# An attention and GEGLU kernel: GELU from ScalarE's table in two batches, column-tiled matmuls between PV bursts, and normalised inputs transposed by DMA

**Chip, cores, metric.** One core of a Trainium2 chip. The metric is the device time of the whole kernel in microseconds (us), the median over repeated runs. Now and then an execution shows a lower granted TensorE clock and takes over 1.5% longer than the fastest of its kernel; it is called *slow*, the others *fast*.

## The reference

```python
xn = layernorm(x)                      # x: 1 x 2048 x 448, bf16
q, k, v = split(xn @ wqkv)             # 16 heads of 28
o = softmax(q @ k.T * 28 ** -0.5) @ v
h = gelu_tanh(xn @ w_gate) * (xn @ w_up)    # 448 -> 1792
out = x + o @ wo + h @ w_down
```

## The kernel before

The program is written by a scheduler in Python: it keeps a clock for each engine, simulates, and emits instructions in the order that the simulation finds. In the traces here every engine, and the queue of DMA issues of SyncE, keeps to its own list and waits for semaphores (below, TensorE stands 12.85 us at one matmul with scores behind it).

Words used below. Tokens come in four blocks of 512. A *tile* is a 128 x 1024 block of scores (two heads x 512 queries, 128 keys); there are 512. Most are exponentiated by ScalarE (*exps*). A *group* is two tiles that VectorE handles by writing bit patterns (`w`, then four `t`), which TensorE multiplies with V four times instead of once. *PV* is the product with V; it uses TensorE as four column tiles of 32.

The GELU, with its scheduling left out (`# ...` marks cuts everywhere):

```python
# g: evicted gate, gu: up * g, both by VectorE
nc.vector.tensor_mul(a, g, g)
nc.vector.tensor_scalar(out=a, in0=a, scalar1=GC1, scalar2=GC0, op0=ALU.mult, op1=ALU.add)
nc.vector.tensor_mul(a, a, g)
nc.scalar.activation(a, a, AF.Tanh, scale=TANH_SCALE)
nc.vector.tensor_scalar(out=a, in0=a, scalar1=0.5, scalar2=0.5, op0=ALU.mult, op1=ALU.add)
nc.vector.tensor_mul(ht, a, gu)
```

Transposes of the normalised inputs of tokens 512 to 2047, and a projection's matmul:

```python
def g_transpose(t0):                       # two token tiles of 128
    tp = aux_tile([P, NDC, 2 * P], BF16, "tp")
    for j in range(2):
        for c in range(NDC):               # four chunks of 112 features
            nc.tensor.transpose(tp[0:DCH, c, j*P:(j+1)*P], xn[:, c*DCH:(c+1)*DCH], ident[:])
    # ... VectorE: xnT[...] = tp

nc.tensor.matmul(ps[:, sl], lhsT=lhsT, rhs=rhs[:, sl], start=start, stop=stop)   # 128 columns
```

The softmax here doesn't subtract the row's maximum and nothing guards it: scores larger than these inputs give would overflow.

## Time and profile before

| | before |
|---|---|
| time, median of 4 runs | 470.06 us (468.82 to 471.89) |
| span in the profile | 466.5 us |
| first exp starts / last exp ends | 12.0 / 458.8 us |
| exps, tanh, table loads between them | 456, 28, 0 |
| ScalarE's waits between first and last exp | 7.7 us |
| tail after the last exp | 7.7 us |

*Waits* here and in all later tables are worked out from the starts of consecutive ScalarE instructions in the trace: what a step takes beyond 0.904 us for an exp and 0.946 us for a tanh or GELU, the steps that the trace shows when nothing waits. Steps into a table load are left out (four, 0.7 us in all in the changed kernel). They include waits too short for the profile to list.

### The profile page before, as it was taken

The numbers are of one execution on the slowest core, as the hardware profiler recorded it, in microseconds if no ns is written. First come the engines' busy times: TensorE is split into PE (matmuls) and PEld (weight loads), VectorE is DVE, ScalarE is ACT, GpSimd is POOL, SyncE is SP. The second block draws the span as 40 slices with busy tenths as digits, with TensorE's granted clock in tenths as the row PEclk, the third lists the DMA queues.
The fourth block names the chain that finished last, engine by engine and source line by source line (L and its number), as shares of the span: only waits on it lengthen the run. The fifth ranks groups of instructions, "written<-read, shape, count | busy, mean of one in ns | idle before, by whom it ended". The sixth has DMA issues, their size and how long they took to land.

```text
span 466.5 us, 9032 instructions
## 1 busy us (share of the span) xinstructions
PE 442.0 (95%) x3468; PEld 156.5 (34%) x3469; DVE 392.9 (84%) x676; ACT 451.8 (97%) x496; POOL 21.1 (5%) x78
## 2 busy tenths in 40 slices
PE   8899999999999999999899999999999899998985
PEld 4333334333223333333233333333233233322431
DVE  6787789789999988999999976899999996697253
ACT  4999999999999999999999999999999999999994
POOL 5602030000000000000000000000000000000000
PEclk9999999999999999999999999999999999999999
DMA  6920112022101002030221000121202100020001
GB/s 161 303 67 2 41 36 64 22 60 59 43 7 39 11 15 57 4 100 22 60 61 42 0 12 21 53 68 52 60 21 54 29 11 12 12 52 1 3 1 39
DMA packets 41051, 20.70 MB, mean 44 GB/s; under 512 B 8240, under 2 KB 41008, under 8 KB 41008
## 3 DMA queue, kind: packets, MB, share of 16 engines
q1 hardware_dynamic: 40112, 19.68, 15.7%
q8 instruction: 27, 0.44, 0.4%
q10 hardware_dynamic: 896, 0.44, 0.3%
q14 instruction: 16, 0.13, 0.1%
HBM read 18.09 MB, written 1.84 MB: 43 GB/s over the span
## 4 chain that ended last, share of the span: by engine, by line
PE 57%; DVE 26%; ACT 8%; issue 4%; DMA 2%; POOL 1%; ACTq 0%; DVEq 0%; SPq 0%; POOLq 0%
PE st L588 15%; PE gups L306 14%; PE ot L636 11%; PE op L306 10%; ACT e L600 7%; DVE w L610 5%; PE pp L306 4%; DVE t L628 4%; DVE gl L394 3%; DVE gu L435 3%; PE pv L306 3%; DVE g L430 3%; DVE otsb L658 2%; DVE w L628 2%; DMA x<-in_A_x_dram 2%
## 5 line engine op out<-in xcount | busy, mean ns | idle before, releaser
L600 ACT ACTIVATE e<-st 128x1024 bf16<-128x1024 f32 x456 | 425.2, 1148 | 2.2 <-PE st L588 2.0
L588 PE MATMUL st<-qT,kT 28*128 28x512 bf16 x1024 | 132.4, 383 | 9.1 <-ACT e L600 7.3
L610 DVE TENSOR_SCALAR w<-st 128x1024 f16<-128x1024 f32 x56 | 68.2, 1219 | 15.6 <-PE st L588 15.0
L588 PEld LDWEIGHTS <-kT 28*128 28x128 bf16 x1024 | 39.0, 91 | 124.4 <-issue 120.3
L636 PE MATMUL ot<-e,va 128*32 128x512 bf16 x912 | 72.5, 383 | 1.3 <-ACT e L600 0.5
L306 PE MATMUL gups<-xnT,wg 112*128 112x512 bf16 (+1 forms) x232 | 62.0, 374 | 1.4 <-DVE kT L343 0.7
L306 PE MATMUL gups<-xnT,wu 112*128 112x512 bf16 (+1 forms) x226 | 61.4, 379 | 2.0 <-DVE qT L343 0.6
L628 DVE TENSOR_SCALAR t<-w 128x2048 uint16<-128x2048 f16 x84 | 54.4, 678 | 0.1
L306 PE MATMUL op<-wd_sb,ht 128*128 128x448 bf16 (+1 forms) x233 | 51.5, 347 | 0.1
L636 PEld LDWEIGHTS <-va 128*32 128x32 bf16 x1360 | 31.1, 95 | 50.8 <-issue 34.9
L430 DVE CAST g<-gups 128x512 bf16<-128x512 f32 x56 | 38.4, 686 | 5.3 <-PE gups L306 4.7
L435 DVE TENSOR_TENSOR gu<-gups,g 128x512 bf16<-128x512 f32 x56 | 38.1, 684 | 2.4 <-PE gups L306 2.1
L413 ACT ACTIVATE gl<-gl 128x1024 bf16<-128x1024 bf16 x28 | 32.9, 1174 | 0.0
L658 DVE TENSOR_TENSOR otsb<-ot,otsb 128x512 f32<-128x512 f32 x36 | 24.6, 684 | 7.1 <-PE ot L636 6.8
L636 PE MATMUL ot<-t,va 128*32 128x512 bf16 x336 | 29.7, 383 | 0.4 <-DVE t L628 0.2
L306 PEld LDWEIGHTS <-wg 112*128 112x128 bf16 x232 | 19.0, 97 | 30.9 <-issue 18.4
L306 PEld LDWEIGHTS <-wu 112*128 112x128 bf16 x226 | 18.3, 97 | 30.8 <-issue 18.8
L306 PEld LDWEIGHTS <-ht 128*128 128x128 bf16 x233 | 19.2, 98 | 24.5 <-issue 12.3
L628 DVE TENSOR_SCALAR w<-w 128x2048 uint16<-128x2048 f16 x28 | 19.3, 690 | 0.7
L394 DVE TENSOR_TENSOR gl<-gl,g 128x1024 bf16<-128x1024 bf16 x28 | 19.2, 685 | 0.3
L394 DVE TENSOR_TENSOR gl<-g 128x1024 bf16<-128x1024 bf16 x28 | 19.1, 684 | 0.2
L394 DVE TENSOR_TENSOR ht<-gl,gu 128x1024 bf16<-128x1024 bf16 x28 | 19.1, 683 | 0.2
(105 smaller groups left out, 289.8 us busy)
## 6 DMA issues: line engine op xcount, KB each, us to landing
wg<-in_B_w_gate_dram SPq DMA_DIRECT2D x28, 224.0 KB
wu<-in_B_w_up_dram SPq DMA_DIRECT2D x28, 224.0 KB
out_dram<-res SPq DMA_DIRECT2D x15, 112.0 KB
wd_sb<-in_B_w_down_dram SPq DMA_DIRECT2D x1, 1568.0 KB
x<-in_A_x_dram SPq DMA_DIRECT2D x3, 448.0 KB
den<-otsb SPq DMA_DIRECT2D x60, 2.0 KB
rr<-recb SPq DMA_DIRECT2D x60, 1.0 KB
wst<-in_A_wqkv_dram SPq DMA_DIRECT2D x2, 392.0 KB
```

What stands on the lines that cost most here:

```text
L306: nc.tensor.matmul(ps[:, sl], lhsT=lhsT, rhs=rhs[:, sl], start=start, stop=stop, skip_group_check=True)
L394: (nc.gpsimd if eng == "POOL" else nc.vector).tensor_mul(out, a, b)
L413: nc.scalar.activation(st["a"][:], st["a"][:], AF.Tanh, scale=TANH_SCALE)
L430: nc.vector.tensor_copy(g[:, k, :], ps[:])
L435: nc.vector.tensor_mul(gu[:, k, :], ps[:], g[:, k, :])
L588: nc.tensor.matmul(st[:, j * QT : (j + 1) * QT], lhsT=kT[(hg, kc // 4)][32 * hh : 32 * hh + Dh, (kc % 4) * P : (kc % 4 + 1) * P], rhs=qT[( ...
L600: nc.scalar.activation(e[:], s_tiles.pop(k)[:], AF.Exp, scale=SCALE)
L610: nc.vector.tensor_scalar(out=w_tiles[g][1][:, 2 * i * QT : 2 * (i + 1) * QT], in0=s_tiles.pop(k)[:], scalar1=128.0 * SCALE * LOG2E, scala ...
L628: nc.vector.tensor_scalar(out=bits, in0=w[:], scalar1=c, scalar2=None, op0=ALU.add)
L636: nc.tensor.matmul(ot[32 * hh : 32 * hh + 32, :], lhsT=va, rhs=rhs, start=(b, hh) not in started, stop=last, tile_position=(0, 32 * hh), s ...
L658: nc.vector.tensor_add(otsb[:], ot[:], otsb[:])
```

## The change

The intent: ScalarE has a GELU, so five VectorE instructions per pair of gate tiles can go; two batches keep the switches of ScalarE's table few; VectorE has time for more groups, ScalarE for fewer exps. Matmuls that follow a PV burst are issued as four column tiles, so that TensorE need not change its mode. And TensorE and VectorE are freed of the transposes of tokens 512 on. The core of the diff:

```diff
+    def f(k, ps): nc.vector.tensor_copy(ht[:, k, :], ps[:])             # gate
+    def f(k, ps): nc.vector.tensor_mul(ht[:, k, :], ps[:], ht[:, k, :]) # up, after the GELU
+    for Q in BATCHES[batch_i[0]]:          # BATCHES = ((0, 1), (2, 3)), 14 activations each
+        for pr in range(NPR):
+            nc.scalar.activation(ht[:], ht[:], AF.Gelu_apprx_tanh)
-    # the chain around tanh
@@ matmuls
+            for m in range(0, P, P // cols):          # cols is 4 next to a PV burst, else 1
+                nc.tensor.matmul(ps[m : m + P // cols, sl], lhsT=lhsT[:, m : m + P // cols], ...,
+                                 **({"tile_position": (0, m)} if cols > 1 else {}))
@@ transposes
-            add(first - 8 + k, [...], lambda t0=t0: g_transpose(t0))
+    def ln_apply_t(t):
+        ln_apply(t)
+        for c in range(NDC):
+            nc.sync.dma_start(xnT[T][:, c, j * P : (j + 1) * P], xn[:, c * DCH : c * DCH + P], transpose=True)
+        xt_at[t] = clock["DVE"] + T_XT     # T_XT = 6000: the scheduler counts on them 6 us later
@@ norms: 1/denominator is broadcast by a DMA through HBM, not by a matmul
@@ limits of the groups
-    D_SLACK = 5; D_END = 2; D_STOP = 40; NL = 6
+    D_SLACK = 20; D_END = 3; D_STOP = 60; NL = 8
```

## The prediction

> **What bounds the kernel now.** I read the head of the page first, then its 40 slices. The columns of the first part are the engine, busy time, share of the span and instructions.
>
> ```profile
> span 466.5 us, 9032 instructions
> PE 442.0 (95%) x3468; PEld 156.5 (34%) x3469; DVE 392.9 (84%) x676; ACT 451.8 (97%) x496; POOL 21.1 (5%) x78
> ...
> DVE  6787789789999988999999976899999996697253
> ACT  4999999999999999999999999999999999999994
> ```
>
> ScalarE is full in every slice but the first and the last. TensorE at 95% looks as full, but its busy time is a union of modelled, overlapping spans; the slices do not tell which of the two sets the pace. So I turned to the timeline of ScalarE (start, length, engine, line, operation, count, and idle time before in brackets).
>
> ```profile
> 11.96 3.77 ACT L600 ACTIVATE e<-st 128x1024 bf16<-128x1024 f32 x4 [0.61 <-PE st L588]
> ...
> 200.72 1.20 ACT L413 ACTIVATE gl<-gl 128x1024 bf16<-128x1024 bf16 x1
> 201.67 16.75 ACT L600 ACTIVATE e<-st 128x1024 bf16<-128x1024 f32 x18
> ...
> 219.07 3.04 ACT L600 ACTIVATE e<-st 128x1024 bf16<-128x1024 f32 x3
> 221.78 1.26 ACT L413 ACTIVATE gl<-gl 128x1024 bf16<-128x1024 bf16 x1
> ...
> 424.65 34.14 ACT L600 ACTIVATE e<-st 128x1024 bf16<-128x1024 f32 x37
> 461.98 0.97 ACT L1292 CAST res<-fa 128x448 bf16<-128x448 f32 x2 [3.18 <-PE fa L1283]
> ```
>
> Start to start gives what an instruction costs when the next follows at once. Three exps take 221.78 - 219.07 = 2.71 us, so 0.903 us each; a tanh takes 201.67 - 200.72 = 0.95 us. The first exp starts at 11.96 and the last ends at 424.65 + 34.14 = 458.79. Between lie 456 exps x 0.903 = 411.8 us and 28 tanh x 0.95 = 26.6 us, 438.4 of 446.8 us. So **ScalarE's instruction count sets the time**: 12.0 us of prologue, 438.4 of work, 8.4 of waits (many under the 0.2 us that the views show as idle), 7.7 of tail. A TensorE that stood in the way would leave more than 2% of waits.
>
> VectorE already takes exps from ScalarE. A group handles two score tiles by writing bit patterns: two w instructions from PSUM, then four terms, each of which TensorE multiplies again. The groups of instructions by line (busy time, mean ns | idle) are:
>
> ```profile
> L610 DVE TENSOR_SCALAR w<-st 128x1024 f16<-128x1024 f32 x56 | 68.2, 1219 | 15.6 <-PE st L588 15.0
> L628 DVE TENSOR_SCALAR t<-w 128x2048 uint16<-128x2048 f16 x84 | 54.4, 678 | 0.1
> ...
> L413 ACT ACTIVATE gl<-gl 128x1024 bf16<-128x1024 bf16 x28 | 32.9, 1174 | 0.0
> ...
> L394 DVE TENSOR_TENSOR gl<-gl,g 128x1024 bf16<-128x1024 bf16 x28 | 19.2, 685 | 0.3
> L394 DVE TENSOR_TENSOR gl<-g 128x1024 bf16<-128x1024 bf16 x28 | 19.1, 684 | 0.2
> L394 DVE TENSOR_TENSOR ht<-gl,gu 128x1024 bf16<-128x1024 bf16 x28 | 19.1, 683 | 0.2
> L403 DVE TENSOR_SCALAR gl<-gl 128x1024 bf16<-128x1024 bf16 x28 | 11.7, 418 | 0.1
> L417 DVE TENSOR_SCALAR gl<-gl 128x1024 bf16<-128x1024 bf16 x28 | 11.6, 419 | 0.3 <-ACT gl L413 0.3
> ```
>
> 56 w make 28 groups, hence 512 - 56 = 456 exps. The last five lines are the GELU written out around tanh, 80.7 us of VectorE.
>
> **What the Trainium skill says.** "ScalarE: Activation LUTs", What happens when an exp ACTIVATE runs: all functions cost the same per element, so a GELU should cost what a tanh does; Table sets, in the same page, puts exp and tanh in one set and gelu in another. The trace agrees for exp and tanh: 28 tanh lie among the exps without one load. The page's What ACT_TABLE_LOAD costs gives 1283 ns plus about 1380 ns of drain. The trace shows the first number and not the second: the load at 8.06 us starts 0.01 us after the ACTIVATE before it ends, takes 1.28 us, and the next starts 0.02 us later. I use 1.28 us. "TensorEngine Tiling (Array Packing)", Key Properties: a change of tiling mode drains TensorE. Agrees: two full matmuls start 0.215 us apart, and a score matmul after one starts 0.31 us after it, so a switch costs 0.1 us. "DMA: Bandwidth & Descriptors", DMA Transpose (X-bar): such a transpose moves 2-byte data to SBUF in multiples of 16 partitions, which fits the padded 128-column reads here; no run of the kernel before shows its latency.
>
> **The change part by part.**
>
> 1. *GELU by table.* The number of ScalarE activations outside the softmax stays 28 and I keep 0.95 us for each: nothing gained there. Two batches (GELU in, Exp back) add 4 loads x 1.28 = 5.1 us. A load also ends the overlap of neighbours (a tanh lasts 1.17 us but costs 0.95), 0.2 us each. **+6.0 us on ScalarE, on the path.** VectorE loses 80.7 us; evictions of gate and up stay (56 + 56 at 0.69 us).
>
> 2. *What the freed VectorE may take.* The gain must come from more groups, and the diff caps them. A group takes quads n and n+2 (a quad is four heads against 128 keys), the next must start at n+3 or later, and the new D_END of 3 wants n+3 in the same block. Blocks have 4, 5 or 6 quads, so one per block at most; before, a block of 6 could hold two. I count blocks: in the first quarter 16 blocks of 4, of which groups begin only once all keys and values are projected. In the trace the first w starts at 108.3 us, by which about 100 exps and some three tiles in stock had gone, so tile 104, quad 52, the 14th block: three blocks left. Second and third quarter 12 each. In the last quarter D_STOP of 60 tiles ends at quad 226, so seven. Sum **34 at most**. The old limits allowed 36 blocks and some second groups, but the lag limit and a VectorE at 98% left 28. VectorE after: 392.9 - 80.7 - 4.1 (copies of PE transposes) + 5 x 5.2 = 334 us, 73%, so nearly all 34 should be taken; I take 33. Five more groups are ten fewer exps: **-9.0 us**.
>
> 3. *Waits of ScalarE.* In two of the stretches with most waits, 220-240 and 360-380 us, VectorE is at 19.6 and 19.8 of 20 us and TensorE falls to 18.2: TensorE waits for PSUM that VectorE has not emptied. With VectorE at 73% this should shrink; new waits can come after a batch. I put 8.4 to 5.5: **-2.9 us**.
>
> 4. *Column tiles, and norms and transposes off TensorE.* In the order of starts in the trace only 55 steps go from a PV to a full matmul and 26 from a full one to a PV: 81 x 0.1 = 8 us of switches that can go, less 0.014 us for each matmul issued as four column tiles. The 15 broadcasts of 1/denominator (0.31 us, 5 us with switches) and the 48 transposes (about 3 us) also go; five groups bring 5 x 12 matmuls at a quarter of 0.226 us, 3.4 us. TensorE gets some 10 us of slack. It isn't the bound: **0 us** directly. During a batch of 14 x 0.95 + 2.8 = 16 us it has up matmuls (first batch) or little (second), and ScalarE does not need it.
>
> 5. *DMA transposes.* Tokens 512 on are first needed at quad 16, tile 32, about 12 + 32 x 0.9 = 41 us; they are normalised near 16 us. Some 25 us of room: 0 us. The norm's extra DMA hop also has room until the last block but one.
>
> Sum: 6.0 - 9.0 - 2.9 = -5.9 us. On 470.65 that gives 464.7; I say **464.5 us**.
>
> **Rivals.**
> - *The table loads eat it all*: with 30 groups instead of 33, or the page's drain (4 x 1.38 = 5.5 us more), the change is worth 0: 469 to 471. For it: the lag and buffer conditions can reject groups. Against: the trace shows no drain, and eight buffers hold two groups.
> - *ScalarE starves less than I allow*: all 34 groups (-10.8 us) and waits down to 2 us (-6.4) give 6.0 - 10.8 - 6.4 = -11.2, so 459.5. For it: waits follow a crowded VectorE. Against: 60-80 us has as long a wait (0.51 us before one exp), ahead of the first group.
> - *TensorE becomes the bound after the batches*: the up matmuls of half the tokens (14 x 8 x 0.23 = 26 us) come in a burst after each batch, those of the last half after 2/3 of the exps, with the output products behind them. My sum for the last 125 us is 53 of scores, PV and switches, 4 of groups, 26 of up, 27 of output products: 110, 88%. If it overflows, the tail grows by some us: 470 to 475.
> - *A slower start*, if transposes queue behind the 1.6 MB of down weights: it would show as ScalarE idle at 35-45 us, +2 to +5 us.
>
> **Range and chances.** The first rival sets the upper end, 470; the second the lower, 459. Two per cent faster is below 461.2, which needs nearly the whole second rival: 0.2. Slower by 2% is over 480, which none reaches but a starved TensorE together with lost groups: 0.03.
>
> **What would show it.** Right: w count near 66 and exps near 446; four more table loads of 1.28 us with no other gap; GELU start to start 0.95 us in two runs of 14; VectorE near 73%; first exp still at 12 us and tail near 7.7 us. Wrong: fewer than 62 w; a GELU that costs more; ScalarE idle beside a batch, at 35-45 us or in the last quarter. The prediction fails outright if TensorE's waits on something other than exps grow to over 10 us of ScalarE idle.

## The result, and the profile after

| | before | after |
|---|---|---|
| time, median of 4 runs | 470.06 us | 512.06 us (510.60 to 514.01) |
| span in the profile | 466.5 us | 512.2 us |
| exps / table loads among them | 456 / 0 | 444 / 4 |
| waits of ScalarE between first and last exp | 7.7 us | 57.8 us |
| tail | 7.7 us | 7.8 us |
| mean granted TensorE clock | 0.999 | 0.952 |

The ratio is 1.089 (95% interval 1.084 to 1.095). A ratio is the mean time of one kernel's fast runs over that of the other's in the same rounds, so it is not quite the ratio of the medians.

The page of the changed kernel, parts 1, 2 and the first group of part 5:

```profile
PE 457.8 (89%) x4382; PEld 162.8 (32%) x4383; DVE 350.9 (68%) x560; ACT 449.0 (88%) x488; POOL 20.3 (4%) x82
...
ACT  4973716964999999899999999999999989999994
...
PEclk9995767996999999999999999999999999999999
...
L552 ACT ACTIVATE e<-st 128x1024 bf16<-128x1024 f32 x444 | 410.5, 1124 | 49.9 <-PE st L540 49.1
```

From the eleventh slice on (128 us) ScalarE is about as full as before. The loss lies in the slices before that: in five of the eight from the third to the tenth ScalarE is idle for 30% of the time or more, and in five of them TensorE's clock is cut. Exps fell by 12 as intended, and 50 us of listed idle time came in their place. Who kept TensorE from bringing the scores? The waits of the changed kernel (engine, with PE for TensorE's matmuls and PEld for its weight loads, line, waited for: us in total, times, longest):

```profile
ACT e L552 <- PE st L540: 49.1, 22, 13.1
...
PEld L285 <- DMA xnT<-xn: 18.9, 11, 7.3
...
PEld L285 <- DMA wg<-in_B_w_gate_dram: 14.1, 3, 13.3
...
PE gate L285 <- DMA wg<-in_B_w_gate_dram: 13.0, 2, 12.8
PE pp L285 <- DMA xnT<-xn: 12.9, 7, 6.6
```

TensorE waited for two DMAs: the transposed inputs `xnT`, and the gate weights `wg`. (A matmul and its weight load can wait for the same thing at once, so the four lines don't add up.) Both are issued from SyncE's queue. Its timeline (SPq), in the columns start, length, queue, line, operation and number:

```profile
17.98 11.17 SPq L791 DMA_DIRECT2D wo_sb<-in_A_wo_dram  x16
29.25 21.12 SPq L807 DMA_TRANSPOSE xnT<-xn  x16
50.47 0.53 SPq L162 DMA_DIRECT2D wg<-in_B_w_gate_dram  x1
58.80 15.74 SPq L807 DMA_TRANSPOSE xnT<-xn  x12
74.64 0.52 SPq L162 DMA_DIRECT2D wg<-in_B_w_gate_dram  x1
```

The 16 transposes of one block take the queue from 29.25 to 50.37 us, 1.3 us each, and a load of gate weights can issue only behind them. TensorE's timeline shows both effects:

```profile
47.81 0.58 PE L285 MATMUL pp<-xnT,wk 112*128 112x512 bf16 x1 [3.01 <-DMA xnT<-xn]
48.98 0.61 PE L285 MATMUL pp<-xnT,wk 112*128 112x512 bf16 x1 [0.58 <-DMA xnT<-xn]
50.24 0.61 PE L285 MATMUL pp<-xnT,wk 112*128 112x512 bf16 x1 [0.65 <-DMA xnT<-xn]
...
77.67 0.61 PE L285 MATMUL gate<-xnT,wg 112*128 112x512 bf16 x1 [12.85 <-DMA wg<-in_B_w_gate_dram]
```

Matmul for matmul, TensorE steps along with the transposes at their pace of 1.2 to 1.3 us; at 77.67 it has stood 12.85 us at a gate matmul whose weights were issued at 74.64. A gate matmul is not urgent, but the scores behind it in TensorE's list are.

The same stretch in both kernels (busy us of PE, PEld, DVE, ACT, POOL, the clock, DMA share, GB/s), first before, then after:

```profile
60.00:82.00 22.00, 20.81 (x161) 8.09 (x158) 19.72 (x43) 21.50 (x24) 3.52 (x13) 1.00 0.18 53
```

```profile
60.00:82.00 22.00, 9.15 (x84) 2.93 (x84) 5.09 (x10) 7.71 (x9) 0.00 (x0) 0.66 0.17 37
```

All the compute engines starve together, while the DMA engines are as little busy as before (17% against 18%): the transposes don't fill the DMA engines, they fill the queue that issues. The clock of 0.66 fits the waits: "TensorE: Matmul & The Clock Gate" (Part 1, The HAM clock gate) of the Trainium skill says that an idle TensorE is set to half rate. The trace agrees: matmuls last 0.61 us after such a wait, against 0.38 to 0.40 otherwise.

### The profile page after: what moved, and what is told of

It is laid out like the page before. It is cut to its first block, busy times and chain, and to the rows that moved or that the text cites. A ratio compares the mean times of both kernels' runs of the same rounds, so it can differ in the third digit from the quotient of the medians.

```text
span 512.2 us, 10844 instructions
## 1 busy us (share of the span) xinstructions
PE 457.8 (89%) x4382; PEld 162.8 (32%) x4383; DVE 350.9 (68%) x560; ACT 449.0 (88%) x488; POOL 20.3 (4%) x82
## 4 chain that ended last, share of the span: by engine, by line
PE 58%; ACT 14%; DVE 10%; DMA 8%; SPq 5%; issue 3%; ACTq 0%; POOL 0%; DVEq 0%; POOLq 0%
PE st L540 15%; ACT e L552 14%; PE ot L588 13%; PE op L285 10%; PE gate L285 6%; PE up L285 6%; SPq L807 5%; PE pp L285 4%; DMA wu<-in_B_w_up_dram 4%; PE pv L285 2%; DVE w L562 2%; DVE t L580 2%; DVE ht L370 2%; PE jp L1055 1%; DMA x<-in_A_x_dram 1%
## 5 line engine op out<-in xcount | busy, mean ns | idle before, releaser
L552 ACT ACTIVATE e<-st 128x1024 bf16<-128x1024 f32 x444 | 410.5, 1124 | 49.9 <-PE st L540 49.1
L285 PE MATMUL gate<-xnT,wg 112*32 112x512 bf16 (+2 forms) x387 | 65.2, 388 | 13.5 <-DMA wg<-in_B_w_gate_dram 13.0
L285 PE MATMUL up<-xnT,wu 112*32 112x512 bf16 (+2 forms) x411 | 57.1, 380 | 8.6 <-DMA wu<-in_B_w_up_dram 6.6
L370 DVE CAST ht<-gate 128x512 bf16<-128x512 f32 x56 | 38.2, 686 | 29.3 <-PE gate L285 28.9
L285 PE MATMUL op<-wd_sb,ht 128*32 128x448 bf16 (+2 forms) x502 | 57.7, 345 | 0.0
L386 DVE TENSOR_TENSOR ht<-up,ht 128x512 bf16<-128x512 f32 x56 | 38.3, 688 | 19.2 <-PE up L285 16.7
L285 PEld LDWEIGHTS <-wg 112*32 112x32 bf16 (+1 forms) x387 | 19.7, 97 | 41.5 <-issue 15.4
L285 PE MATMUL pp<-xnT,wk 112*32 112x512 bf16 (+1 forms) x130 | 20.7, 406 | 13.0 <-DMA xnT<-xn 12.9
L285 PEld LDWEIGHTS <-wu 112*32 112x32 bf16 (+1 forms) x411 | 20.3, 96 | 37.6 <-DMA wu<-in_B_w_up_dram 13.1
L285 PEld LDWEIGHTS <-ht 128*32 128x32 bf16 (+1 forms) x502 | 21.4, 97 | 19.0 <-issue 6.8
L1121 ACT ACTIVATE ht<-ht 128x1024 bf16<-128x1024 bf16 x28 | 26.7, 1041 | 0.0
```

What stands on the lines that cost most here:

```text
L285: nc.tensor.matmul(ps[m : m + P // cols, sl], lhsT=lhsT[:, m : m + P // cols], rhs=rhs[:, sl], start=start, stop=stop, skip_group_check=Tr ...
L370: nc.vector.tensor_copy(ht[:, k, :], ps[:])
L386: nc.vector.tensor_mul(ht[:, k, :], ps[:], ht[:, k, :])
L552: nc.scalar.activation(e[:], s_tiles.pop(k)[:], AF.Exp, scale=SCALE)
L1121: nc.scalar.activation(ht[:], ht[:], AF.Gelu_apprx_tanh)
```

## The experiments

Theory A: the transposes' time in SyncE's queue makes keys and weights late. Rival B: another part starves ScalarE. Rival C: only the scheduler's estimate of 6 us is wrong, since TensorE stands still at whatever it was told to do first. More came up on the way. "Against before" is the ratio with its 95% interval; spans, waits and tails are from each run's profile.

| run | against before | exps | span | waits | tail |
|---|---|---|---|---|---|
| changed kernel | 1.089 (1.084 to 1.095) | 444 | 512.2 | 57.8 | 7.8 |
| e1_pe_transpose | 0.997 (0.992 to 1.003) | 444 | 468.3 | 13.5 | 8.3 |
| e1_again | 0.999 (0.994 to 1.004) | 444 | 468.2 | 13.4 | 8.3 |
| e7_before_dma_tr | 1.137 (1.130 to 1.144) | 452 | 533.6 | 59.2 | 26.6 |
| e2_weights_pool_queue | 1.097 (1.092 to 1.102) | 444 | 514.4 | 58.6 | 7.9 |
| e3_txt26 | 1.136 (1.131 to 1.142) | 444 | 533.5 | 75.8 | 11.1 |
| e8_half_transposes | 1.211 (1.206 to 1.217) | 444 | 570.7 | 116.1 | 7.8 |
| e18_one_per_tile | 1.012 (1.006 to 1.018) | 444 | 474.6 | 19.9 | 7.5 |
| e17_first_block_dma | 1.024 (1.021 to 1.027) | 444 | 480.1 | 25.9 | 7.8 |
| e9_spaced_pf | 1.010 (1.007 to 1.013) | 444 | 474.3 | 19.5 | 7.8 |
| e11_wu_prefetch | 0.989 (0.987 to 0.992) | 444 | 463.8 | 8.7 | 8.3 |
| e12_best | 0.990 (0.986 to 0.993) | 444 | 463.6 | 9.1 | 8.3 |
| e19_one_per_tile_pf | 1.002 (0.997 to 1.006) | 444 | 467.9 | 14.4 | 7.6 |
| e4_no_coltile | 1.036 (1.031 to 1.041) | 444 | 485.3 | 24.5 | 14.2 |
| e13_no_coltile_pf | 1.017 (1.011 to 1.022) | 444 | slow | slow | slow |
| e5_tanh_no_load | 1.018 (1.014 to 1.022) | 444 | slow | slow | slow |
| e14_tanh_pf | 1.005 (1.000 to 1.009) | 444 | 470.3 | 14.4 | 15.1 |
| e6_more_groups | 1.039 (1.035 to 1.043) | 438 | 489.2 | 27.7 | 20.5 |
| e15_more_groups_pf | 1.020 (1.015 to 1.025) | 438 | 478.5 | 16.7 | 20.8 |

The profiles of e5 and e13 fell into the slow state (clocks 0.926 and 0.75), so their spans are not used; their ratios rest on their fast runs.

### Undo the transposes: e1_pe_transpose

```diff
+        for k in range(2):
+            add(first - 8 + k, [...], lambda t0=t0: g_transpose(t0))
-            ln_at_time(..., lambda t=4 * g + k: ln_apply_t(t))
+            ln_at_time(..., lambda t=4 * g + k: ln_apply(t), [("xn", 4 * g + k)])
```

> The changed kernel with one part undone: the inputs of tokens 512 on are transposed by TensorE again (48 transposes, 6 copies by VectorE), all else stays. Theory A (the 48 DMA transposes, 1.2 to 1.4 us of the SyncE queue each, make the keys and whatever stands behind them in that queue late): ScalarE's idle time of 50 us falls under 8 us, the clock is back at 1.00 in every stretch, exps stay 444, and the time is 461 to 467. Rival B (another part, such as column tiles, the new order of gate and up or the broadcast through HBM, starves ScalarE): it stays over 490.

Measured: 469.70 us, waits of 13.5 us (7.2 us of them listed as idle time, as expected), clock 0.999, 444 exps. Undoing this one part takes away 42 of 42 us, so the DMA transposes are the cause, and B falls as the main one. How they do the harm is for the other runs. The time is 3 us above the range given: something else, smaller, is left (see e11).

### The transposes alone: e7_before_dma_tr

The kernel before with `ln_apply_t` and what it needs:

```diff
-            xn_g[t // 4] = ltile(..., [P, 4, D], BF16, "xn")
+            g = xn_g[t // 4] = ltile(..., [P, 4, D + 16], BF16, "xn")   # padding, set to 0 by GpSimd
-        for k in range(2):
-            add(first - 8 + k, [...], lambda t0=t0: g_transpose(t0))
+    def ln_apply_t(t): ...       # as in the change, four DMA transposes; T_XT = 6000
-            ln_at_time(p0 + 8 + k, 335, lambda t=4 * g + k: ln_apply(t), [("xn", 4 * g + k)])
+            ln_at_time(p0 + 8 + k, 335, lambda t=4 * g + k: ln_apply_t(t))
```

> The kernel before with the one part alone: DMA transposes in place of TensorE's, with the change's padding and its estimate of 6 us. Theory A: ScalarE idles 30 us or more between 30 and 140 us and the time is 500 to 520, though GELU, column tiles and norms are those of before. Rival B: 468 to 474.

Measured: 535.90 us. It was expected at 500 to 520; the waits, 59.2 us, are of the expected kind and size (0 to 140 us hold 48 of them), and the rest is a tail of 26.6 us: the trace has TensorE at output products until 524 us, 17 us past the last exp. (That the scheduler's clock no longer matches the chip would explain it; this was not tested.) So the part alone is enough for the loss, and 1.137 is more than the changed kernel's 1.089.

### Another queue for weights: e2_weights_pool_queue

```diff
-            nc.sync.dma_start(w[:], ...)        # gate and up weights; wo the same
+            nc.gpsimd.dma_start(w[:], ...)
```

> The changed kernel with its DMA transposes, but the gate, up and output weights are loaded from the GpSimd queue, so that they don't stand behind the transposes nor the transposes behind them. If the order in the one queue is the larger part of theory A, the waits for gate weights (13 + 14 us) go, the first transposes issue near 25 instead of 29 us, and the time falls to 480 to 492. If the transposes' own time (16 x 1.3 = 21 us per 512 tokens, with keys needed at 41 us) is the larger part, it stays at 495 to 508. Rival B: no change, 512.

Measured: 516.60 us, above every range given. This one doesn't decide, because its edit brought a fault of its own: GpSimd too keeps to its list, and it computes the inverse deviations of the norms. In this run it stood 188 us in total at loads that wait for gate matmuls, and the first transposes issued at 31.4 us instead of 29.3. What its trace does show: TensorE's gate matmuls waited 2.3 us for weights instead of 13.0, the projections 19.9 us for `xnT` instead of 12.9, and ScalarE's waits stayed (58.6 us). Whether the one queue or the transposes' length does more harm had to be asked otherwise (e9, e17).

### An honest estimate: e3_txt26

```diff
-    T_XT = 6000
+    T_XT = 26000
```

> The changed kernel, with one number of the scheduler changed: it counts on transposed inputs 26 us after the norm instead of 6. No instruction is added; TensorE's order is built for what the trace shows. Theory C (only the wrong estimate hurts, as TensorE works in order and stops at a matmul that is not ready): most of the idle time goes, 470 to 480. Theory A without C: keys of tokens 512 on are late whatever the order, and gate weights stay behind the transposes in the queue, so 490 to 512.

Measured: 534.67 us, slower than the changed kernel. Told that inputs come late, the scheduler put gate matmuls ahead in TensorE's list, and just their weights stand behind the transposes in the queue, which the scheduler does not model: TensorE waited for `wg` three times, up to 15.9 us. But the longest wait of ScalarE in this run, 26.95 us before the exp at 86.63 us, is of the scheduler's own making. It filled the time with matmuls on zeros (`jp`), and on the chip they ran when the block's 16 transposes had all been issued (by 50.1 us):

```profile
63.14 19.22 PE L1055 MATMUL jp<-va,zl 128*128 128x512 bf16 x43
```

So mending the number alone mends nothing, but this run is no clean test of rival C. As the only cause C falls for other reasons: in the changed kernel the first block's last transpose issues at 49.1 us, after its keys are due at 41, in whatever order TensorE works; and the 12.85 us for gate weights don't come from the 6 us, as the scheduler counts no time for loads of weights at all. As a part it stays open: TensorE stood at transposed inputs from 32.6 us on, with the scores of 8 of the first 32 tiles, which need none of them, still behind in its list.

### By bytes or by instruction: e8_half_transposes and e18_one_per_tile

e8 cuts each transpose into two of 64 tokens; e18 lays the four chunks of 112 features padded to 128 columns in one tile and transposes the whole 128 x 512 at once:

```diff
 e8:
+            for h in range(0, P, P // 2):
+                nc.sync.dma_start(xnT[T][:, c, j*P + h : j*P + h + P//2], xn[h : h + P//2, c*DCH : c*DCH + P], transpose=True)
 e18:
-        for c in range(NDC):
-            nc.sync.dma_start(xnT[T][:, c, j*P : (j+1)*P], xn[:, c*DCH : c*DCH + P], transpose=True)
+        nc.sync.dma_start(xnT[T][:, :, j*P : (j+1)*P], xn, transpose=True)
```

> The changed kernel with each DMA transpose of 128 tokens cut into two of 64: 96 instead of 48, the same bytes. If the 1.2 us of the queue that each takes goes by its bytes, they take 0.6 to 0.7 us, 16 pairs still 21 us, and the time is 505 to 520. If it is a cost of the instruction, 32 take about 40 us for each 512 tokens, and the time rises to 550 or more.

> The changed kernel with one DMA transpose for each 128 tokens in place of four: the four chunks lie padded to 128 columns in one tile, so 12 instructions instead of 48 move the same blocks. e8 showed that halving the bytes left the 1.2 us of the queue as it was. If the cost is the instruction's, 4 of them take some 5 to 8 us for each 512 tokens instead of 21, all blocks are there before their keys are needed, and the time falls from 512 to 466 to 472, like e1. If four times the bytes take four times as long, it stays at 505 or more.

Measured: 570.94 and 476.32 us. The durations (min/median/max in ns, then first and last start) of the issues in the changed kernel, e8 and e18:

```profile
L807 SPq DMA_TRANSPOSE xnT<-xn x48: 1093/1228/2022, 29.3 to 118.8; - x48
```

```profile
L808 SPq DMA_TRANSPOSE xnT<-xn x96: 1090/1226/2184, 29.2 to 174.9; - x96
```

```profile
L810 SPq DMA_TRANSPOSE xnT<-xn x12: 1188/1203/2299, 29.0 to 76.2; - x12
```

Half the bytes or four times the bytes, the median is 1.2 us. In these three runs the cost is one of the instruction. With 12 of them instead of 48 the changed kernel loses 36 of its 42 us, with the DMA transposes still in it; a block's four take 6.34 us instead of 21.1. This is the strongest evidence for the mechanism: the same data on the same path, only fewer issues. (It does not set the queue's time apart from rival C, since with four issues for a block the scheduler's 6 us come nearly true.) e18 missed its range of 466 to 472 by 4 us.

### The deadline: e17_first_block_dma and e9_spaced_pf

Both stand on e11 (below). e17 transposes only tokens 512 to 1023 by DMA; e9 only tokens 1024 to 2047, normalised earlier, with the four instructions of each token tile 5.4 us from the next.

```diff
 e17: T is the block of 512 tokens, g the same for the norms
-        for k in range(2):                          # g_transpose
+        for k in range(0 if T == 1 else 2):
+            # ln_apply_t if g == 1, else ln_apply
 e9
-    ln_p0 = {1: 1, 2: 14, 3: 32}
+    ln_p0 = {1: 1, 2: 9, 3: 30}
-        for k in range(2):                          # g_transpose
+        for k in range(2 if T == 1 else 0):
+            # ln_apply if g == 1, else
+            ln_at_time(p0 + 8 + 4 * k, 335, lambda t=4 * g + k: ln_apply_t(t))
```

> e11 with DMA transposes for tokens 512 to 1023 only (16 of 48). Normalised by 29 us, transposed by 50 us, needed at 41 us. Theory A: one block of stalls between 30 and 75 us of the three that the changed kernel has, 13 to 22 us of ScalarE idle, time 1.017 to 1.036. If the harm comes from all three adding up in the queue alone: under 1.0.

> e11 with DMA transposes for tokens 1024 to 2047 only (32 of 48), each four of them 5.4 us from the next, and TensorE's for tokens 512 to 1023. Keys of the former are first needed at about 70 and 100 us, and no other DMA stands more than some 5 us behind them. Theory A (the transposes are harmful as they end after the keys are needed and hold up the queue): the time is e11's, 0.985 to 0.995. If DMA transposes harm in another way (their traffic, or TensorE's order without its own transposes): over 1.02.

Measured: 481.77 and 475.25 us. e17 is as expected: 25.9 us of waits against e11's 8.7, 17 us for one block. e9 missed: 1.010, not 0.985 to 0.995. Nothing waited there for transposed inputs, and after 65 us ScalarE waits as little as in e11. The miss is one wait of 7.1 us at 59 us: eight transposes issued in a row (10.1 us of the queue from 41.88), not the four that I had in mind, and a load of gate weights got out only at 52.10 behind them; TensorE stood 5.59 us for it. So both halves of theory A are there, each by itself: keys that come after their deadline (e17), and other DMAs held up in the queue (e9).

### The waits left in e1: e11_wu_prefetch

In e1 each of the two GELU batches is followed by up matmuls in one go. TensorE's timeline in e1 after the first batch:

```profile
150.64 3.82 PE L285 MATMUL up<-xnT,wu 112*32 112x512 bf16 x64 [1.34 <-DMA wu<-in_B_w_up_dram]
155.40 3.82 PE L285 MATMUL up<-xnT,wu 112*32 112x512 bf16 x64 [0.93 <-DMA wu<-in_B_w_up_dram]
160.18 1.91 PE L285 MATMUL up<-xnT,wu 112*32 112x512 bf16 x32 [0.96 <-DMA wu<-in_B_w_up_dram]
162.02 0.40 PE L540 MATMUL st<-qT,kT 28*128 28x512 bf16 x4
```

Two buffers for the up weights are too few for a burst. (The same stretch gives the price of column tiles: each group of four, the work of one full matmul, starts 0.23 us after the one before; untiled matmuls start 0.215 us apart.)

```diff
-    w = wgupool.tile(..., tag=nm)
+    w = wgupool.tile(..., tag=nm, bufs=3 if nm == "wu" else 2)
-        load_w("wu", n + 1)
+        for m in range(1, 3):
+            load_w("wu", n + m)
```

> e1 with one more buffer for the up weights, loaded two pairs ahead. In e1 the up matmuls of a batch stop for their weights every second pair (some 4.75 us for 3.8 us of matmuls) and TensorE, which works in order, brings the next scores only at 162 us, 3.7 us after the last table load has ended. Theory D (that is where the waits after each batch come from): the waits after the two batches, 2.6 and 2.3 us, fall under 1 us each, the time by 3 to 4 us against e1 (ratio 0.988 to 0.992). Rival: the scores are late because TensorE's program has too many up matmuls ahead of them; then nothing changes.

Measured: 465.71 us, 0.989; the waits after the two batches are 1.1 and 0.3 us, the first just over the 1 us expected, all waits 8.7. Theory D holds.

### The best version: e12_best, and the whole change mended: e19_one_per_tile_pf

e12 is e11 without the padding, which nothing needs once TensorE transposes:

```diff
-            g = xn_g[t // 4] = ltile(..., [P, 4, D + 16], BF16, "xn")
-            nc.gpsimd.memset(g[:, :, D : D + 16].bitcast(F32), 0.0)
+            xn_g[t // 4] = ltile(..., [P, 4, D], BF16, "xn")
```

e19 is e18 with the edit of e11, line for line.

> e11 without the padding of the normalised tiles, which only DMA transposes need and whose memset stands in GpSimd's queue ahead of the first transposes: first exp 0.5 to 0.8 us earlier, 0.986 to 0.989. Faster than both kernels, by about 1.2% against the one before.

> e18 with the up weights loaded two pairs ahead, as in e11. The whole change, with its two queue stalls mended: 461 to 466, ratio 0.982 to 0.990, as TensorE is rid of 48 transposes that e11 and e12 still do. If transposes by DMA bring nothing once they do no harm, it equals e12's 0.990. If they are still late, it is over 1.0.

Measured: e12 465.76 us, first exp at 12.08 instead of 12.75, but the time equals e11's, and 0.990 is just outside the range: the 0.7 us gained at the start show up as waits of 0.85 us in the first 20 us. It beats both kernels, by 1.0% and by 9%. e19 missed: it has 470.47 us, as slow as the kernel before. It waits 14.4 us, 5.3 more than e12, spread over the first 110 us; one wait of 1.4 us at 53 us is again a gate weight load behind transposes, the others I did not settle. So DMA transposes in a quarter of the instructions do no great harm here, but they bring nothing either: e19 is still 1.2% slower than e12 (1.002 against 0.990, intervals apart).

### Column tiles, table loads, more groups: e4, e5, e6, and e13, e14, e15

Each edit was made twice: on e1, then on e11, because e4 to e6 had longer waits for up weights than e1 and ran on another chip.

> The changed kernel with TensorE's transposes (e1) and no column tiles: projections, gate, up and output matmuls are full 128-column ones again. My prediction's step 4 (8 us of switches on an engine that is not the bound, 0 us on the time): within 1% of e1's 0.997. If column tiles help ScalarE by freeing TensorE, it is 1 to 3% slower than e1 and ScalarE's waits grow by 5 us or more; if the four-fold instructions hurt, it is 1% faster or more.

> Wrong result on purpose: e1 with tanh in place of the GELU in the two batches, so no table load, and the scheduler told so. The same 28 activations of 0.95 us. If a switch costs the load's 1.28 us and little else, it is 5 to 6 us faster than e1 (1.1 to 1.3%, ratio near 0.985). With the drain that the page on ScalarE gives, 10 us faster (2.2%). If the loads hide in waits that are there anyway, less than 3 us.

> e1 with the old limits for groups (a group may begin with two quads left in its block, and up to 40 tiles before the end); the build has 438 exps, 6 fewer. By instruction count 5.4 us faster than e1 (ratio 0.986). If waits for VectorE or TensorE take it back, ScalarE's waits rise from e1's 13.5 us by that much and the time is e1's or worse.

> e1 unchanged, on the chip of the three runs beside it. e4 to e6 ran on another chip than e1, and in each of them the waits for up weights were longer than in e1 (longest 3.2 to 4.2 us against 1.8). If that is the chip, e1 shows it here too: 474 us or more, with a tail over 10 us. If it belonged to what e4 to e6 changed, e1 stays at 469 to 470.

Measured: e4 488.06, e5 480.81, e6 489.94 us, all slower than e1 by 2 to 4%: all three missed what I had expected of them. e1_again on a third chip: 469.63 us. That does not clear the chip of e4 to e6, on which e1 itself never ran (e11 ran on it without such waits, but e11 has the third buffer). So the runs on e11 below have to decide; they ran on the third chip, e11 on that of e4 to e6, and are compared by their ratios against before.

```diff
 e13: no column tiles
-        v = bool(n) and (mode[0] == "V" or mode[0] == "S" and v_soon(start))
+        v = False
-        return 0 if mode[0] == "V" and not fixed else switch("F")
+        return switch("F")
 e14: wrong result on purpose, no table load
-                nc.scalar.activation(ht[:], ht[:], AF.Gelu_apprx_tanh)
+                nc.scalar.activation(ht[:], ht[:], AF.Tanh)          # and T_TABLE = 0
 e15
-    D_END = 3; D_STOP = 60
+    D_END = 2; D_STOP = 40
```

> e11 (TensorE's transposes, up weights loaded two pairs ahead) without column tiles; e4 mixed this with the weight waits. My prediction: column tiles are worth 0 us, so 0.985 to 0.994 like e11's 0.989. Rival: TensorE is nearly full, and 10 us more of switches end as ScalarE waits or as a longer tail: 0.998 or more.

> Wrong result on purpose: e11 with tanh for GELU, no table load. If a load costs 1.28 us and the broken overlap, 4 to 6 us faster than e11 (ratio 0.977 to 0.981). If TensorE's work sets the end now, as the tail of 17 us in e5 hints, no gain: 0.986 or more.

> e11 with the old limits for groups, 438 exps instead of 444. By instruction count 5.4 us faster than e11 (0.978). If TensorE, which has 12 more column-tile matmuls for each group, has no room, waits and tail rise by more than that and it is as slow as e11 or slower.

Measured: 478.32, 471.92 and 479.24 us against e11's 465.71, all of them misses of the expectation that I held first. e14 is the telling one: its four loads are gone, yet its last exp ends at 455.2 us as in e11 (455.6), since 5.7 us of waits have come, and then the tail is 15.1 us instead of 8.3. Not all of that is TensorE's work. After the second batch TensorE stood for up weights, whose next loads were issued only from 362.59 us on, after four `den` transfers; the longest wait of ScalarE in this run comes behind these matmuls:

```profile
367.55 8.84 PE L285 MATMUL up<-xnT,wu 112*32 112x512 bf16 x124 [2.69 <-DMA wu<-in_B_w_up_dram]
```

```profile
377.10 78.13 ACT L553 ACTIVATE e<-st 128x1024 bf16<-128x1024 f32 x85 [3.87 <-PE up L285]
```

In e15 ScalarE's last wait names what stands in that tail:

```profile
ACT res L1290 <- PE fa L1281: 16.0, 1, 16.0
```

ScalarE has finished and waits 16 us for TensorE. In neither run did a shorter ScalarE shorten the kernel: TensorE's work was then not done. This suggests, but does not show, that after the change TensorE is about as full as ScalarE. And the column tiles are worth much in this kernel: without them e13's ratio is 1.017 against 0.989, about 13 us of 466. One caution: each of these edits moves the scheduler's clocks, so that the whole order of TensorE's work differs, and in e14 weights come late too; how much of the 6 to 13 us is work and how much a worse order is not separated, and e13 left no trace of a fast run.

## Why the prediction was wrong

The predicted 464.5 us, with a range to 470, met 512.06. By its own steps:

**Step 5, DMA transposes at 0 us, is the one that failed.** It put the normalised inputs at 16 us and the deadline at 41, "some 25 us of room". Two numbers in it were wrong. The scheduler's time starts near the first exp at 12 us, so the inputs were normalised at 25 to 29 us; then 16 loads of the output weights kept the queue until 29.25. Both could be read in the trace of the kernel before, which has its loads of the output weights in the queue from 15.93 to 30.73 us and the first of the block's norms at 25.41:

```profile
25.41 0.40 DVE L273 TENSOR_SCALAR xn<-x,mean,rstd 128x448 bf16<-128x448 bf16 x1
```

And the step priced no issue time at all: 16 transposes x 1.3 us = 21 us. The first block's were ready at 50.4, nine after the deadline, and the same 16 issues came again for each of the two later blocks. It also looked at the transposes only as something to wait for. In an in-order queue they are something to wait *behind*, and a single gate load behind them cost 12.85 us of TensorE. The fourth rival, a slower start with ScalarE idle at 35 to 45 us, came nearest: it has the transposes waiting behind weights, but neither their own 21 us nor weights waiting behind them. I gave it 2 to 5 us where 44 were lost (57.8 us of waits against e1's 13.5), and I left it out of the range. The words "no run of the kernel before shows its latency" stood beside the transpose; that was the reason to widen the range. The sign that I had named for an outright failure, over 10 us of ScalarE idle from TensorE's waits on something other than exps, is what came.

**Step 1, GELU and loads: +6.0 us, right.** Four loads of 1.28 us, GELUs in two runs of 14 at 13.4 us each. (The page says that functions cost the same per element under Step-by-step, just below the heading that the prediction names.)

**Step 2, groups: right.** At most 34 were counted, 33 taken; the build has 34 and 444 exps, 10.8 us less of ScalarE.

**Step 3, waits shrink to 5.5 us: not so.** Even with the queue stalls mended (e12) they are 9.1 us, more than before's 7.7. Less work on VectorE did not shorten them.

**Step 4, column tiles at 0 us on the path: failed in its reasoning.** It said of TensorE "It isn't the bound", because ScalarE was full. Without column tiles the kernel is 2.8% slower (e13), and e14 and e15 suggest that the two engines are nearly balanced. The test behind the claim, that a TensorE in the way would leave more than 2% of waits, was never measured: e11 waits 8.7 of 443 us, 2.0%, and taking 5 us of table loads off ScalarE (e14) gained nothing. The error did not falsify the sum, since column tiles were in the change.

**The sum without step 5.** Take 12.1 us of prologue, 444 x 0.904 + 28 x 0.946 + 4 x 1.28 = 433.0, e12's waits of 9.1 and tail of 8.3: 462.5 us, and e12's span is 463.6. This shows only that the pieces add up, as the waits and the tail are read from e12 itself. That the predicted 464.5 us lies 1.3 us under e12's 465.76 is in part luck: the groups gave 1.8 us more than booked, the waits came out 3.6 us higher, and e12 has TensorE's transposes and loads up weights further ahead, neither of which the change has.

## What to carry to other kernels

Price a DMA in three ways: when its data land, how long its issue holds the queue, and who stands behind it there; a queue that issues in order starved every compute engine here while the DMA engines were 17% busy. Count instructions before bytes: the same transposes in a quarter of the instructions gave back 36 of 42 us. And an engine at 97% does not make one at 95% free: before a saving on the fuller one is booked, ask whether the other could finish earlier too.

## What the Trainium skill lacked or had wrong

- "DMA: Bandwidth & Descriptors", DMA Transpose (X-bar): the section lists constraints, but no time that an SBUF to SBUF transpose holds the issuing queue on this chip (a table in the page's part on trn3 has cycles for "previous generations" as a whole). The runs show a median of 1.2 us for 64 x 128, 128 x 128 and 128 x 512 elements alike (e8, the changed kernel, e18).
- "Advanced Engine Details and Errata", X-Bar Transpose (TRN2): "TRN2 transpose DMAs are as fast as regular DMAs". The lines beside it are about bandwidth, which no run here measures; for the issuing queue the sentence does not hold. A transpose of 128 x 128 elements held it 1.2 us, a load of gate weights of seven times the bytes 0.31 to 0.53 us (27 of 28 loads in the changed kernel).
- "DMA: Bandwidth & Descriptors", Rules for kernel authors, advises issuing a DMA early and waiting late. It lacks the other side: what is issued early holds up what is issued after it, here by up to 21 us for 16 transposes.
- "ScalarE: Activation LUTs", What ACT_TABLE_LOAD costs: the load of 1283 ns is right; the drain of about 1380 ns beside it shows in no trace here. In e1 a load lasts 1.28 us and the next activation starts 1.29 to 1.30 us after the load's start.
- "TensorEngine Tiling (Array Packing)": it presents column tiles for small matrices only. Here full 128-column matmuls cut into four column tiles ran at about 0.23 us instead of 0.215, and spared mode switches of 0.1 us (starts 0.31 us apart instead of 0.215); without them the kernel was 2.8% slower (e13, whose order of work differs too).
